# The last 256 columns of an FNet and SwiGLU kernel: SiLU, product and sum in two halves, one half's sum on GpSimd

## The chip, the cores and the metric

The kernel runs on one core of a Trainium2 chip. The metric is the device time of one execution in microseconds (us); the time given for a kernel is the median of its runs. A core has five engines that run their own instruction streams: TensorE (PE in the profile; its weight loads are PEld), VectorE (DVE), ScalarE (ACT), GpSimd (POOL) and SyncE (SP). They wait for one another on semaphores. Transfers are issued by SyncE or GpSimd (SPq and POOLq in the profile) and carried out by 16 DMA engines.

## The reference

The input x has 2048 rows (time) of 640 columns. It is normalized along its rows, goes through a Fourier mixing and through a gated feed-forward layer, and the two are multiplied and added to x:

```
xn = layernorm(x)                                            # 2048 x 640
s  = dft_seq_re @ (xn @ dft_hid_re.T) - dft_seq_im @ (xn @ dft_hid_im.T)
h  = silu(xn @ w_gate) * (xn @ w_up)                         # 2048 x 1536
g  = silu(h @ w_down)                                        # 2048 x 640
return x + s * g
```

All arrays are float32.

## The kernel before

Everything is float32, and TensorE gets each operand in two parts: a high part (ScalarE rounds it, in `split`) and a low part (VectorE takes the difference). A product of two such operands is three matmuls, high by high, high by low and low by high (`mm3`). The large products are cut into quarters and multiplied by a scheme of seven products instead of eight (`strassen`); what doesn't fit the quarters (the fifth block of 128 of the 640 columns) is computed directly, in the results named `"d1"` and `"d2"`.

The stages stand in this order at the end of the kernel's main function: four sweeps of the sequence transform (`seq`), two of the hidden transform (`hid_s`), which leave s in DRAM as `y_dram`, and then for each of two pairs of time blocks (j = 0 and 1) the gate and up products (`gate_up`) and the down product (`down`). A time block c has 512 columns of the transposed output, `out`, which is 640 x 2048.

The down product for j = 1 is the end of the kernel. There `strassen` is called with `end` set, and its last product is taken apart by the inner function `alone`: the first 256 columns of the direct block, then two banks of 512 columns for the quarter 21, then the last 256 columns of the direct block. After each of them its result is written by `result`, so that the last of these calls is `result("d2", ..., at=256, w=256)`. It handles 128 rows and 256 columns.

In `result` the buffers have the names `yb` (a piece of s, read back from `y_dram`), `res` (a piece of x, read from the transposed input `xt`) and `fin` (the piece of the output). For a direct block of j = 1 the work is: ScalarE takes SiLU of the PSUM bank into `fin` (line 1319), VectorE multiplies it by `yb` (line 1323), VectorE adds `res` (line 1330), and SyncE issues the store (line 1332). The two loads are issued by SyncE some time ahead (lines 1313 and 1315).

Nothing of this is issued where it is written. `pl.post`, `pl.prod` and `pl.step` put each instruction on a list (`Plan`) with the keys that it reads and writes, and `Plan.schedule` runs them in a planned time: matmuls (`step`) set the clock, and the others get a lane for each engine and one for all DMAs. The planner prices an instruction by its columns: columns/1183 + 0.09 us on ScalarE, columns/960 + 0.075 on VectorE, columns/500 + 0.2 on any other engine (line 92), with 0.2 us between an instruction and one that needs it. What follows a matmul (`post`) is put at its earliest time. A load (`prod`) is put as late as its first reader allows, less a reserve; loads are handled from the last to the first, and each takes the free place of the DMA lane next to its due time. The list is then sorted by planned time, and that is the order of each engine's instructions. `Plan.place` gives the buffers addresses in the arenas `hl` and `raw` by their planned lifetimes: it tries several orders and keeps the one in which buffers that follow one another at an address leave the most time between them. A buffer that is placed where another has just ended makes its first instruction wait for the other's last. All of `fin`, `yb` and `res` lie in `raw`.

All instructions of the main function are recorded under line 82 of the profile, the line of the helper through which they are issued, so groups are told apart by tile and shape.

Of the kernel before, what the change touches and what calls it, by code (L numbers as in the profile page):

```python
# [11 lines left out]
AF = mybir.ActivationFunctionType  # L12
ALU = mybir.AluOpType

P = 128
S, D, F = 2048, 640, 1536
TC = 512
# [261 lines left out]
def tile_fnet_swiglu(  # L279
# [16 lines left out]
    nc = Probe(tc.nc)  # L296
# [5 lines left out]
    pl = Plan()  # L302
# [8 lines left out]
    ps = psum.tile([P, 8, TC], F32, name="ps")  # L311
# [3 lines left out]
    def raw(name, a=0, n=None):  # L315
        o, (arena, size) = where[name], pl.size[name]
        n = size - a if n is None else n
        over = arena == "raw" and o >= RAW_KB * 256 - 8
        return space["raw3" if over else arena][:, o + a - over * (RAW_KB * 256 - 8):][:, :n]

    def hl(name, i, a=0, n=None):

        key = name, "hl"[i]
        o, n = where[key], pl.size[key][1] - a if n is None else n
        over = bisect(HL_AT, o) - 1
        return space[("hl", "hl2", "hl3")[over]][:, o + a - HL_AT[over]:][:, :n]
# [21 lines left out]
    def both(dst, *subs):  # L348
        return [(dst, p, s) for s in (subs or (0,)) for p in "hl"]
# [24 lines left out]
    def pair(b):  # L374
        return ps[:, b[0]:b[0] + len(b), :]
# [4 lines left out]
    def pkeys(b):  # L380
        return [("ps", i) for i in b]
# [6 lines left out]
    def combine(dst, b, other, op, a=0, after=0.0):  # L388
        n = len(b) * TC
        pl.post(lambda: nc.vector.tensor_tensor(wide(raw(dst, a, n)), pair(b), wide(raw(other)), op=op),  # L390
                [*pkeys(b), (other, 0)], [(dst, a)], after)
# [881 lines left out]
    def down(j):  # L1273
        names = {}

        def fetch(p, g):
            n = 768 if p[0] == "p" else 384
            name = names[p, g] = pl.buf(("Td", j, p, g), "hl", 2 * n)
            for i in range(2):
                pl.prod(14 - 4 * g, lambda i=i: nc.sync.dma_start(  # L1280
                    hl(name, i).bitcast(F32), d_dram[p, g][:, i * n:i * n + n]), [("dd", p, g, i)], [(name, "hl"[i], 0)])

        def top(p):
            for g in range(2):
                fetch(p, g)
            return (lambda g, kk, e, i: hl(names[p, g], i, kk * 256 + e * P, P)), (lambda g: both(names[p, g]))

        def dop(h):
            p = f"d{h}"
            if (p, 0) not in names:  # L1290
                for g in range(2):
                    fetch(p, g)
            return (lambda g, kk, e, i: hl(names[p, g], i, kk * P, P)), (lambda g: both(names[p, g]))

        def get(q, g):
            name = ("h", j, q % 10 - 1, q // 10)
            return name, 3 * g * TC, (name, "all", g)

        for half in range(2):
            for c in (1, 2):  # L1300
                name = ("h", j, half, c)
                for g in range(2):
                    pl.alias[name, "all", g] = [(name, (3 * g + i) * TC) for i in range(3)]

        def result(q, b, other, op, at=0, w=TC, e=0):
            half, e0 = (int(q[1]), 4) if isinstance(q, str) else (q // 10, 2 * (q % 10 - 1) + e)
            n = len(b) * w
            c = j + 2 * (half - 1)
            late = 0 if j and q in ("d2", 21) else 4
            yb, name, res = (pl.buf((what, j, q, at, e), "raw", n) for what in ("yb", "fin", "res"))  # L1310
            part = lambda ap: ap.rearrange("p (a b) -> p a b", b=w)
            fold = j == 0
            fold or pl.post(lambda: nc.sync.dma_start(
                part(raw(res)), xt[c, e0:e0 + len(b), :, at:at + w].rearrange("k p t -> p k t")), [], [(res, 0)], -8)
            pl.post(lambda: nc.sync.dma_start(
                part(raw(yb)), y_dram[c, e0:e0 + len(b), :, at:at + w].rearrange("k p t -> p k t")),
                [("yd", c, e0 + i) for i in range(len(b))], [(yb, 0)], -8)
            if other is None:
                pl.post(lambda: nc.scalar.activation(part(raw(name)), pair(b)[:, :, at:at + w], AF.Silu), pkeys(b), [(name, 0)])
            else:  # L1320
                combine(name, b, other, op)
                pl.post(lambda: nc.scalar.activation(raw(name), raw(name), AF.Silu), [(name, 0)], [(name, 0)])
            pl.post(lambda: nc.vector.tensor_tensor(raw(name), raw(name), raw(yb), op=ALU.mult),
                    [(name, 0), (yb, 0)], [(name, 0)], late)
            if fold:
                pl.post(lambda: nc.gpsimd.dma_start(
                    part(raw(name)), xt[c, e0:e0 + len(b), :, at:at + w].rearrange("k p t -> p k t"), accum_op=ALU.add),
                    [], [(name, 0)], late + 1)
            else:
                pl.post(lambda: nc.vector.tensor_tensor(raw(name), raw(name), raw(res), op=ALU.add),  # L1330
                        [(name, 0), (res, 0)], [(name, 0)], late + 1)
            pl.post(lambda: (nc.sync if j and q in ("d2", 21) else nc.gpsimd).dma_start(
                out[e0 * P:(e0 + len(b)) * P, c * TC + at:c * TC + at + w].rearrange("(k p) t -> p k t", p=P),
                part(raw(name))), [(name, 0)], [], late + 3, 8)

        strassen(("down", j), [3, 3], get, top, dop, result, j == 1)


# [83 lines left out]
```

## Time and profile before

| | |
|---|---|
| time, median of 3 runs | 969.77 us (969.72 to 969.93) |
| time of the profiled execution | 969.83 us |
| span of the profiled execution, first to last instruction | 967.6 us |
| granted TensorE clock, share of full speed | 0.999 |
| TensorE busy | 961.7 us (99%) |
| VectorE, ScalarE, GpSimd busy | 734.6, 488.6, 121.3 us |
| last matmul starts | 963.03 us |
| last store issued | 964.71 us |

Times in the profile's views are microseconds from the start of the span. A row of the timeline has an instruction's start, its duration, the engine, the line, the operation, output and input by the program's names, their number, and in brackets the idle time of the engine just before, with what ended it. A row of the groups has the number of instructions, their busy time in all and the mean duration of one in ns, then the engine's idle time before them. The chain is the work that ended last, followed back from the end to what released each step.

### The profile page before, as it was taken

Reading aid. Unit: us, or ns where it says so; the run is one execution under the profiler, and the core shown is the slowest. Engines: PE = TensorE matmul, PEld = TensorE weight load, DVE = VectorE, ACT = ScalarE, POOL = GpSimd, SP = SyncE. Lnnn points to the kernel's source line nnn. Section 1 sums busy time; section 2 is a strip of 40 time slices with the busy share of each in tenths; the row PEclk is TensorE's granted clock in tenths of the full one; section 3 lists DMA queues with packets and bytes.
Section 4 is the critical chain, followed back from the end, with each engine's and each line's share of the span. In section 5 each row is a group of like instructions: output and inputs, shape, how many; then the busy total and the mean of one; then the engine's idle time right before and its main releaser. Section 6 shows DMA issues by size and latency. Waiting matters only on the chain.

```text
span 967.6 us, 11521 instructions
## 1 busy us (share of the span) xinstructions
PE 961.7 (99%) x4235; PEld 792.0 (82%) x4235; DVE 734.6 (76%) x932; ACT 488.6 (50%) x676; POOL 121.3 (13%) x184
## 2 busy tenths in 40 slices
PE   9999999999999999999999999999999999999998
PEld 5888888888888888888888888888888888888887
DVE  7889668757774687676987898999978666666775
ACT  5686445454545455544356555563446444444341
POOL 1460211011101110111100211210002000000000
PEclk9999999999999999999999999999999999999999
DMA  9997848494938497778673374439699330105793
GB/s 352 283 249 215 233 147 229 152 271 106 231 109 255 109 236 263 208 196 253 170 213 131 141 265 155 168 136 289 222 292 256 99 133 4 55 1 163 240 346 131
DMA packets 64056, 186.50 MB, mean 193 GB/s; under 512 B 6528, under 2 KB 10368, under 8 KB 64000
## 3 DMA queue, kind: packets, MB, share of 16 engines
q1 hardware_dynamic: 45952, 125.45, 39.0%
q0 software_dynamic: 18048, 60.32, 24.2%
q8 instruction: 33, 0.54, 0.2%
q14 instruction: 23, 0.19, 0.1%
HBM read 151.39 MB, written 34.36 MB: 192 GB/s over the span
## 4 chain that ended last, share of the span: by engine, by line
PE 99%; DMA 0%; DVE 0%; ACT 0%; issue 0%; DVEq 0%; ACTq 0%
PE ps L82 99%; DMA xn<-in_x 0%; DVE raw L82 0%; DVE bst L82 0%; DVE sm L82 0%; ACT raw L82 0%; ACT sm L82 0%; DVE mv L82 0%; DVEq L82 0%; ACTq L82 0%
## 5 line engine op out<-in xcount | busy, mean ns | idle before, releaser
L82 PE MATMUL ps<-hl 128*128 128x512 f32 (+1 forms) x3258 | 780.1, 388 | 0.0
L82 PEld LDWEIGHTS ps<-hl 128*128 128x128 f32 x3258 | 610.1, 188 | 126.6 <-DVE hl L82 0.6
L82 DVE TENSOR_TENSOR hl<-raw,hl 128x1024 fp32r<-128x1024 f32 (+5 forms) x360 | 346.5, 994 | 134.3 <-ACT hl L82 94.4
L82 ACT ACTIVATE hl<-raw 128x1024 fp32r<-128x1024 f32 (+6 forms) x416 | 325.0, 826 | 170.3 <-DVE raw L82 84.8
L82 PE MATMUL ps<-hl,hl 128*128 128x512 f32 (+1 forms) x954 | 259.9, 388 | 0.0
L82 ACT ACTIVATE raw<-ps 128x512 f32<-128x512 f32 (+1 forms) x144 | 97.9, 681 | 231.4 <-PE ps L82 225.2
L82 PEld LDWEIGHTS ps<-hl,hl 128*128 128x128 f32 x954 | 179.0, 188 | 36.9
L82 DVE TENSOR_TENSOR raw<-raw 128x1024 f32<-128x1024 f32 (+7 forms) x216 | 178.6, 849 | 19.8 <-ACT raw L82 15.5
L82 DVE TENSOR_TENSOR raw<-ps,raw 128x512 f32<-128x512 f32 (+1 forms) x95 | 77.2, 814 | 48.4 <-PE ps L82 47.6
L82 DVE TENSOR_TENSOR raw<-raw,raw 128x512 f32<-128x512 f32 (+3 forms) x50 | 44.2, 892 | 6.5 <-ACT raw L82 4.3
L82 ACT ACTIVATE hl<-xn 128x1024 fp32r<-128x1024 f32 (+3 forms) x61 | 42.2, 723 | 13.6 <-PE ps L82 9.1
L82 POOL DMA_DIRECT2D p_dram<-raw x24 | 16.4, 686 | 251.4 <-DVE raw L82 215.7
L82 ACT ACTIVATE raw<-raw 128x512 f32<-128x512 f32 (+1 forms) x30 | 21.5, 718 | 46.7 <-DVE raw L82 46.7
L82 DVE TENSOR_TENSOR hl<-xn,hl 128x1024 fp32r<-128x1024 f32 (+3 forms) x50 | 40.8, 833 | 4.0 <-PE ps L82 3.9
L82 POOL DMA_DIRECT2D raw<-in_cs x36 | 32.5, 984 | 57.7 <-DMA raw<-in_cs 29.1
L82 DVE SCALAR_TENSOR_TENSOR hl<-raw,hl 128x256 fp32r<-128x256 f32 (+4 forms) x56 | 32.7, 586 | 4.0 <-ACT hl L82 4.0
L82 POOL DMA_DIRECT2D out<-raw x10 | 6.9, 689 | 226.6 <-DVE raw L82 197.3
L82 POOL DMA_DIRECT2D d_p<-hl x28 | 15.2, 543 | 71.4 <-ACT hl L82 59.6
L82 ACT ACTIVATE xn<-xn,sm,rowst 128x640 f32<-128x640 f32 (+1 forms) x16 | 14.1, 906 | 5.3 <-DVE sm L82 3.6
L82 DVE BATCH_NORM_STATS2 bst<-xn 128x6 f32<-128x320 f32 x32 | 13.7, 479 | 4.0 <-DMA xn<-in_x 4.0
L82 POOL DMA_DIRECT2D y_dram<-raw x12 | 8.2, 683 | 64.6 <-DVE raw L82 46.2
L82 POOL DMA_DIRECT2D raw<-p_dram x8 | 10.1, 1267 | 44.7 <-DVE raw L82 26.3
(42 smaller groups left out, 84.3 us busy)
## 6 DMA issues: line engine op xcount, KB each, us to landing
raw<-in_cs SPq DMA_DIRECT2D x84, 512.0 KB, 7.0
hl<-d_p SPq DMA_DIRECT2D x56, 384.0 KB, 5.0
raw<-in_cs POOLq DMA_DIRECT2D x36, 512.0 KB, 9.8
raw<-in_wb SPq DMA_DIRECT2D x24, 640.0 KB, 4.7
d_p<-hl POOLq DMA_DIRECT2D x28, 384.0 KB, 4.0
p_dram<-raw POOLq DMA_DIRECT2D x16, 512.0 KB, 4.4
raw<-p_dram SPq DMA_DIRECT2D x8, 768.0 KB, 8.5
xn<-in_x SPq DMA_DIRECT2D x16, 320.0 KB, 9.8
```

The costliest lines, as they stand in the source:

```text
L82: return real(*args, **kw)
```

## The change

In the last call of `result` (the condition `j and at` holds for no other), SiLU is taken in two halves of 128 columns, each an instruction of ScalarE out of PSUM. Each half is multiplied by its half of `yb` on VectorE. Then the first half of `res` is added on GpSimd, and the second on VectorE. The store is one, of both halves, from SyncE, and waits for both sums. The two loads and their leads, and the planned time of the store, are as before; the products and sums have no planned delay of their own any more (`late` and `late + 1` before, that is 0 and 1 us).

```diff
@@ -1315,6 +1315,19 @@
             pl.post(lambda: nc.sync.dma_start(
                 part(raw(yb)), y_dram[c, e0:e0 + len(b), :, at:at + w].rearrange("k p t -> p k t")),
                 [("yd", c, e0 + i) for i in range(len(b))], [(yb, 0)], -8)
+            if j and at:
+                m = w // 2
+                for i in range(2):
+                    pl.post(lambda a=i * m: nc.scalar.activation(
+                        raw(name, a, m), ps[:, b[0], at + a:at + a + m], AF.Silu), pkeys(b), [(name, i)])
+                for other, op in ((yb, ALU.mult), (res, ALU.add)):
+                    for i in range(2):
+                        add_on = nc.vector if other is yb or i else nc.gpsimd
+                        pl.post(lambda a=i * m, other=other, op=op, add_on=add_on: add_on.tensor_tensor(
+                            raw(name, a, m), raw(name, a, m), raw(other, a, m), op=op), [(name, i), (other, 0)], [(name, i)])
+                pl.post(lambda: nc.sync.dma_start(out[e0 * P:e0 * P + P, c * TC + at:c * TC + at + w], raw(name)),
+                        [(name, 0), (name, 1)], [], late + 3, 8)
+                return
             if other is None:
                 pl.post(lambda: nc.scalar.activation(part(raw(name)), pair(b)[:, :, at:at + w], AF.Silu), pkeys(b), [(name, 0)])
             else:
```

## The prediction

> **What bounds the kernel now.** I read the page first: the span, the busy times, the shares of the chain that ended last.
>
> ```profile
> span 967.6 us, 11521 instructions
> PE 961.7 (99%) x4235; PEld 792.0 (82%) x4235; DVE 734.6 (76%) x932; ACT 488.6 (50%) x676; POOL 121.3 (13%) x184
> PE 99%; DMA 0%; DVE 0%; ACT 0%; issue 0%; DVEq 0%; ACTq 0%
> ```
>
> TensorE sets the time. The change touches no matmul, so what it can move is what stands behind the last one. For that I read the end of the chain in order of time (start, duration, what), then SyncE's row in the timeline of the tail, the landing of that store, and what is left of the span behind it.
>
> ```profile
> 6.46 956.86 PE ps L82 x4224
> 963.32 0.02 issue
> 963.34 0.39 ACT raw L82
> 963.74 0.02 issue
> 963.76 0.44 DVE raw L82
> 964.20 0.02 issue
> 964.22 0.42 DVE raw L82
> ...
> 964.71 0.33 SPq L82 DMA_DIRECT2D out<-raw  x1
> ...
> out<-raw SPq DMA_DIRECT2D x1, 128.0 KB, 1.9
> ...
> 964.64:967.60 2.96, 0.00 (x0) 0.00 (x0) 0.00 (x1) 0.00 (x0) 0.00 (x0) 0.63 0.19 68
> ```
>
> TensorE runs one unbroken piece to 963.32. Behind it stand SiLU (963.34 to 963.73), the product (963.76 to 964.20), the sum (964.22 to 964.64), the store's issue 0.07 later at 964.71, its landing 1.9 later, and the rest of the span. So the piece that the change edits is 964.64 − 963.34 = **1.30 us**, 0.13% of the time. The 2.96 us from 964.64 on hang on the store, which stays one store of the same 128 KB; they move with it and keep their length.
>
> **The prices that the trace has.** Rows by shape (mean ns behind the busy time), then one pair of ScalarE instructions from the timeline that don't depend on each other:
>
> ```profile
> L82 ACT ACTIVATE raw<-ps 128x512 f32<-128x512 f32 x113 | 67.4, 598 | 161.0 <-PE ps L82 155.2 <-DVE raw L82 2.3 <-ACT hl L82 1.9
> L82 ACT ACTIVATE raw<-ps 128x256 f32<-128x256 f32 x2 | 0.8, 375 | 1.6 <-PE ps L82 1.6
> L82 ACT ACTIVATE hl<-xn 128x128 fp32r<-128x128 f32 x8 | 2.4, 294 | 0.0
> L82 DVE TENSOR_TENSOR raw<-raw 128x512 f32<-128x512 f32 x37 | 25.6, 691 | 14.0 <-ACT raw L82 12.8
> L82 DVE TENSOR_TENSOR raw<-raw 128x256 f32<-128x256 f32 x68 | 28.1, 419 | 2.1 <-ACT raw L82 2.0
> L82 DVE TENSOR_TENSOR hl<-xn,hl 128x128 fp32r<-128x128 f32 x8 | 2.2, 273 | 0.0
> ...
> 952.17 1.06 ACT L82 ACTIVATE raw<-raw 128x1024 f32<-128x1024 f32 x1 [7.16 <-DVE raw L82]
> 953.14 0.37 ACT L82 ACTIVATE raw<-ps 128x256 f32<-128x256 f32 x1
> ```
>
> A half costs more than half. SiLU of 128 columns out of PSUM: 598 for 512 and 375 for 256 give 0.87 ns a column and 0.26 us for 128; the nearest row of that size (from SBUF) says 0.29. I take 0.27. A product or sum of 128 on VectorE: 419 − (691 − 419)/2 = 283, the row of that size says 273; I take 0.28. Two ScalarE instructions in a row overlap by 952.17 + 1.06 − 953.14 = 0.09.
>
> **The change, part by part.** *SiLU in halves*: adds one instruction. First 963.34 to 963.61, second 963.52 (the 0.09 of overlap) to 963.79; the first half is ready 0.12 earlier than the whole was, the second 0.06 later. *Products in halves*, both on VectorE: the gap behind ScalarE is 0.03 to 0.04, so the first runs 963.65 to 963.93. The second waits for the second SiLU (963.79 + 0.03 = 963.82) and stands behind the first in VectorE's queue. What VectorE and GpSimd do to one another there is read from the one place where both work hard, about 42 us:
>
> ```profile
> 41.07 0.33 DVE L82 BATCH_NORM_AGGREGATE mv<-bst 128x2 f32<-128x12 f32 x2
> 41.49 0.18 POOL L82 TENSOR_SCALAR sm<-mv 128x2 f32<-128x2 f32 x1 [1.89 <-DVE mv L82]
> 41.76 0.72 POOL L82 TENSOR_TENSOR sm<-sm 128x2 f32<-128x2 f32 x1
> 42.55 1.23 DVE L82 TENSOR_TENSOR hl<-raw,hl 128x1024 fp32r<-128x1024 f32 x1 [1.15 <-ACT hl L82]
> 42.57 1.26 POOL L82 TENSOR_SCALAR sm<-mv 128x2 f32<-128x2 f32 x1
> 43.69 1.22 DVE L82 TENSOR_TENSOR hl<-raw,hl 128x1024 fp32r<-128x1024 f32 x1
> 43.80 1.17 POOL L82 TENSOR_TENSOR sm<-sm 128x2 f32<-128x2 f32 x1
> 44.83 1.67 DVE L82 BATCH_NORM_STATS2 bst<-xn 128x6 f32<-128x320 f32 x4
> 45.88 0.20 POOL L82 TENSOR_TENSOR sm<-sm,rowst 128x2 f32<-128x2 f32 x1
> 46.10 0.93 ACT L82 ACTIVATE xn<-xn,sm,rowst 128x640 f32<-128x640 f32 x1 [1.72 <-POOL sm L82]
> ...
> L82 POOL MEMSET z<- 128x512 bf16 x1 | 0.5, 524 | 0.3 <-POOLq L1412 0.3
> L82 POOL MEMSET sm<- 128x4 f32 x2 | 0.1, 104 | 0.0
> ```
>
> Two VectorE instructions without a wait between them overlap by 42.55 + 1.23 − 43.69 = 0.09, so the second product runs 963.84 to **964.12**; without that overlap it would run 963.95 to 964.23, which I keep as the late end.
>
> *First half's sum on GpSimd.* Three things have a row. GpSimd started 41.49 − (41.07 + 0.33) = 0.09 after VectorE released it, so it can begin at 963.93 + 0.09 = 964.02. An operation of two columns is 0.20, and ScalarE took over 46.10 − 46.08 = 0.02 after it. And it is held: the same kind of two-column scaling took 0.18 with VectorE idle and 1.26 beside a VectorE instruction with two tensors from SBUF, ending 42.57 + 1.26 − (42.55 + 1.23) = 0.05 behind it; the next one ended 43.80 + 1.17 − (43.69 + 1.22) = 0.06 behind the next such instruction. Beside the statistics, which read one tensor, it took 0.20. The second product reads two tensors and starts first (963.84 against 964.02), so I count the GpSimd sum as held to 964.12 + 0.05, and its columns after that.
>
> [...]
>
> The price of a column of a GpSimd sum has no row. Low end: the fill, (524 − 104)/508 = 0.83 ns, one write a column. High end: three such turns, two reads and a write, 2.5 ns. I take two turns, 1.65 ns: one for each of the two tensors read, with the write beside them. 126 columns beyond the two already in the row are then 0.21 us (0.10 to 0.31).
>
> [...]
>
> *Second half's sum on VectorE* is ready at 964.12 + 0.02 = 964.14 and takes 0.28. [...] If GpSimd goes first it ends at 964.17 + 0.21 = 964.38 and VectorE's ends at 964.66. If VectorE goes first, it ends at 964.42 and GpSimd's at 964.42 + 0.05 + 0.21 = 964.68. The order hardly matters: **964.66 to 964.68 against 964.64, +0.03 us**. With 0.10 to 0.31 for the columns it is 964.55 to 964.78, with the late product up to 964.89: −0.09 to +0.25.
>
> *The store* now waits for two engines. Nothing is queued behind it on SyncE. GpSimd's last work is an earlier store, and so is what SyncE did before:
>
> ```profile
> 957.11 0.72 POOL L82 DMA_DIRECT2D out<-raw  x1 [8.13 <-DVE raw L82]
> ...
> 954.94 0.87 SPq L82 DMA_DIRECT2D raw<-y_dram  x2
> 955.86 0.42 SPq L82 DMA_DIRECT2D raw<-in_xt  x1
> 963.30 0.34 SPq L82 DMA_DIRECT2D out<-raw  x1
> ```
>
> So GpSimd has been free for 6 us when the sum reaches it, and no store is behind it. The product's and the sum's other operands (y and x) are issued by 956.28, over 7 us ahead of their readers: an operand wanted 0.1 or 0.2 earlier costs nothing, and without that cover it would cost what is missing of its landing. The edits to the plan (three more instructions, no other DMA) go with this.
>
> **Sum.** Time of the profiled execution 969.83 (span 967.6 and 2.2 around it) + 0.03 = 969.86. The median of the three runs is 0.06 lower, so on its scale 969.80. I predict 969.85, between them. What a measurement here can tell from no change is about 0.2%, 1.9 us; the whole edited piece is 1.30, so not even its disappearance would show.
>
> **Rivals.**
>
> 1. *No hold.* The sums run side by side: GpSimd 964.02 + 0.20 + 0.21 = 964.43, VectorE 964.42, so 0.21 faster, 969.6. For it: VectorE's two instructions at 42 us lost nothing (1.23 and 1.22) though GpSimd worked beside them. Against it: GpSimd's own 1.26 and 1.17.
>
> 2. *Slower: GpSimd ends the chain.* Place: its sum, behind VectorE's second sum. From (964.64 − 964.47)/126 = 1.35 ns a column on, GpSimd ends later than the sum did before; it leaves the forecast's bounds once a column costs over 2.5 ns or the start takes longer than the 0.20 of the two-column rows. Upper price: the power at 41.76 took 0.72 for two columns with VectorE idle; 964.42 + 0.72 + 0.31 = 965.45, 0.8 later, 970.6. [...] Against: the other two-column rows, 0.18 to 0.20 unheld.
>
> 3. *The halves are not apart*: if the first product waits for both SiLUs, it runs 963.82 to 964.10, the second ends at 964.29, and the two sums one after the other at 964.29 + 0.26 + 0.28 = 964.83, 0.2 later, 970.0. The code names the halves apart, which speaks against it.
>
> 4. *The plan moves elsewhere.* Loads and buffers are placed by planned times, and x's due time moves by what the code's own prices give: before (0.306 + 0.2) + (0.342 + 0.2) = 1.05 behind the SiLU's start, after 0.81. If buffers of the body are placed anew and one load comes late by its whole landing, some 3 to 7 us:
>
> ```profile
> raw<-in_xt SPq DMA_DIRECT2D x1, 128.0 KB, 2.8
> raw<-in_cs SPq DMA_DIRECT2D x84, 512.0 KB, 7.0
> ```
>
> then it is 972.6 to 976.8. Against it: all that moves is at the very end.
>
> **Chances and range.** Forecast 0.55, no hold 0.20, GpSimd ends the chain 0.15, halves not apart 0.05, plan moved 0.05. The first four stay within 0.2%; of the last I give 0.03 to slower, 0.01 to faster (a buffer placed better) and the rest to no difference: faster 0.01, same 0.96, slower 0.03. The range takes in the first four: low 969.45 (0.22 below the median and the runs' spread of 0.1), high 970.6 (rival 2's upper price).
>
> **What would show it.** In the changed profile: the last matmul still at 963.0 and the one piece of TensorE unbroken; two SiLUs of about 0.27; two VectorE products of 0.28 that overlap; a GpSimd sum that ends only behind a VectorE instruction; a last sum between 964.5 and 964.9; the store's issue 0.07 behind it. The forecast is wrong if the GpSimd sum ends before the second product does, if it takes over 0.7, or if TensorE's piece has a gap that wasn't there.

## The result, and the profile after

The changed kernel takes 970.96 us (median of 22 runs, 970.84 to 971.54), the kernel before 969.83 in the same number of runs (969.52 to 970.09). The ratio is 1.0013, 95% interval 1.0007 to 1.0019: slower by 1.1 us. That is less than the 0.2% that the prediction took as what can be told from no change, but clear of the spread, and above the predicted range (969.45 to 970.6).

First the end of the chain in the changed kernel (start, duration, what; TensorE's last unbroken piece begins at 16.25 here, after a wait of 0.2 us), then three rows of its timeline: the second SiLU, GpSimd's sum and the store.

```profile
16.25 946.93 PE ps L82 x4193
963.18 0.02 issue
963.21 0.29 ACT raw L82
963.49 0.02 issue
963.52 0.20 DVE raw L82
963.72 0.01 issue
963.73 0.30 DVE raw L82
964.02 0.02 issue
964.04 0.45 DVE raw L82
```

```profile
963.38 0.27 ACT L82 ACTIVATE raw<-ps 128x128 f32<-128x128 f32 x1
...
963.90 0.44 POOL L82 TENSOR_TENSOR raw<-raw 128x128 f32<-128x128 f32 x1 [6.21 <-DVE raw L82]
...
964.56 0.33 SPq L82 DMA_DIRECT2D out<-raw  x1
```

The edited piece is as forecast: 963.21 to 964.49, that is 1.28 us against 1.30 before. GpSimd's sum ends at 964.34, VectorE's at 964.49, the store is issued 0.07 behind it. TensorE even ended 0.14 earlier in this execution. So the loss stands behind the store, where the kernel's work is over. The rows for that stand under the line of the program's end, which isn't a line of the kernel's work: L1431 in the changed kernel, L1418 in the kernel before. A row has the number of instructions, the shortest, median and longest duration in ns, and the start of the first and the last; a DRAIN stands at the end of each engine's part. The changed kernel, then the kernel before:

```profile
L1431 SPq EVENT_SEMAPHORE  x12: 17/28/28, 964.9 to 969.0; - x12
L1431 POOLq EVENT_SEMAPHORE  x4: 17/17/17, 967.9 to 969.0; - x4
L1431 POOLq DRAIN  x3: 93/188/4015, 963.9 to 968.7; - x3
L1431 SPq DRAIN  x3: 7/7/7, 966.8 to 968.1; - x3
L1431 ACTq EVENT_SEMAPHORE  x2: 17/17/17, 968.0 to 969.0; - x2
```

```profile
L1418 POOLq EVENT_SEMAPHORE  x4: 17/17/17, 966.8 to 967.5; - x4
L1418 POOLq DRAIN  x3: 46/93/5734, 957.1 to 967.2; - x3
L1418 SPq DRAIN  x3: 7/7/7, 966.7 to 967.0; - x3
L1418 ACTq EVENT_SEMAPHORE  x2: 17/17/17, 966.9 to 967.6; - x2
```

All five engines have drains under this line (in the changed kernel TensorE's weight loads from 960.9 on, ScalarE from 963.2, VectorE from 964.1). Behind the first of each come GpSimd's semaphore instructions, which I read as the collection of the engines; ScalarE's first comes 0.1 us behind GpSimd's first in both kernels (966.9 behind 966.8, 968.0 behind 967.9). In both kernels SyncE's part is done by 966.7 to 966.9, and the store has landed (1.9 behind its issue at 964.71 before, 2.1 behind 964.56 now). Before, GpSimd goes on at 966.8, at once. In the changed kernel it goes on at 967.9, since its own drain, which begins with the sum at 963.9 and takes 4.015, ends only then. The kernel before has the same drain, 5.734 long, but behind the last store that GpSimd issues, 957.1 to 962.8, under the matmuls. The 1.1 us between 966.8 and 967.9 are the 1.1 us of the result. (The span grew by 1.5, from 967.6 to 969.1. The 0.4 beyond the 1.1 lie between GpSimd's first semaphore instruction and the end, and the times of the two profiled executions do not have them: 969.83 and 970.87, 1.0 apart.)

### The profile page after: what moved, and what is told of

Its sections match the earlier page's. It is cut to its first block, busy times and chain, and to the rows that moved or that the text cites. A ratio compares the mean times of both kernels' runs of the same rounds, so it can differ in the third digit from the quotient of the medians.

```text
span 969.1 us, 11527 instructions
## 1 busy us (share of the span) xinstructions
PE 961.2 (99%) x4235; PEld 792.1 (82%) x4235; DVE 734.8 (76%) x933; ACT 488.6 (50%) x677; POOL 122.3 (13%) x185
## 4 chain that ended last, share of the span: by engine, by line
PE 98%; DMA 1%; DVE 0%; SPq 0%; ACT 0%; issue 0%
PE ps L82 98%; DMA raw<-in_cs 1%; SPq L82 0%; DVE hl L82 0%; DVE raw L82 0%; ACT xn L82 0%; ACT hl L82 0%; ACT raw L82 0%
## 5 line engine op out<-in xcount | busy, mean ns | idle before, releaser
L82 ACT ACTIVATE raw<-ps 128x512 f32<-128x512 f32 (+2 forms) x145 | 98.0, 678 | 232.3 <-PE ps L82 226.1
L82 DVE TENSOR_TENSOR raw<-raw 128x1024 f32<-128x1024 f32 (+8 forms) x217 | 178.9, 847 | 18.0 <-ACT raw L82 15.6
L82 POOL DMA_DIRECT2D raw<-in_xt x6 | 6.9, 1296 | 72.2 <-DVE raw L82 72.1
```

Of the source, the lines that this page charges most:

```text
L82: return real(*args, **kw)
```

## The experiments

Theory A: the end waits for GpSimd's closing drain, some 3.5 us behind GpSimd's last instruction. Rival B: a fetch of instructions falls into the tail because the program got longer. Rival C: the hold between VectorE and GpSimd, or a store that waits for two engines.

**The halves without GpSimd.**

```diff
-                        add_on = nc.vector if other is yb or i else nc.gpsimd
+                        add_on = nc.vector
```

> The halves as in the changed kernel, but both sums on VectorE; GpSimd's last instruction is again the store of the row at 957. Theory A (the end waits for GpSimd's closing drain, which takes some 3.5 us behind GpSimd's last instruction): that drain ends near 962.8 under the matmuls as before, the tail is 0.1 shorter than the kernel before, 969.7. Rival B (a fetch of instructions that falls into the tail because the program is longer): three instructions more as in the changed kernel, so about 970.9. Rival C (the hold between VectorE and GpSimd, or a store that waits for two engines): both are gone, 969.7; this run does not tell A from C.

Measured: 969.68 us against 969.77 (ratio 1.0001, 0.9992 to 1.0010). Its drain, the first SiLU in its chain, and the second half's sum on VectorE:

```profile
L1431 POOLq DRAIN  x3: 46/93/5742, 957.1 to 967.3; - x3
```

```profile
963.33 0.28 ACT raw L82
```

```profile
964.25 0.28 DVE L82 TENSOR_TENSOR raw<-raw 128x128 f32<-128x128 f32 x1
```

The drain is back under the matmuls and the 1.1 us are gone, with three instructions more than before: B falls for the length of the program. The packets of instructions don't go with the loss either: on queue 14 the pages count 24 in the changed kernel, 24 in this run, which lost nothing, and 23 both in the kernel before and in the next run, which lost 1.6 us. The sum takes 0.28 here and 0.45 beside GpSimd's, so the hold is there, and costs 0.17. The piece is 963.33 to 964.53, 1.20 us: the halves alone save 0.1, which the time can't show.

**A GpSimd instruction that nobody waits for.**

```diff
+            if j and at:
+                pl.post(lambda: nc.gpsimd.tensor_tensor(sm[:, 0, :2], raw(name)[:, :2], raw(name)[:, 2:4], op=ALU.add),
+                        [(name, 0)], [("idle", 0)], late + 2)
```

> The kernel before, with one GpSimd instruction of two columns behind the last sum, whose result nobody reads; the store does not wait for it. Theory A: it runs near 964.8 to 965.0, the closing drain ends some 3.5 later at 968.4, against 966.8 where SyncE is done, so the time is 1.6 to 2.0 above the kernel before: 971.4 to 971.9. Rival B: one instruction more, between no difference and 1.1: 969.8 to 970.9. Rival C: nothing on the store's path waits, 969.8.

Measured: 971.38 us (ratio 1.0016, 1.0007 to 1.0025).

```profile
964.69 0.18 POOL L82 TENSOR_TENSOR sm<-raw 128x2 f32<-128x2 f32 x1 [6.97 <-DVE raw L82]
```

```profile
L1421 POOLq DRAIN  x3: 46/102/3742, 964.7 to 968.9; - x3
L1421 SPq DRAIN  x3: 7/7/7, 966.6 to 968.7; - x3
```

Two columns that no store waits for cost 1.6 us. VectorE and the store are those of the kernel before, and SyncE is done at 966.6 (966.7 there): C falls as the cause of the loss. The drain ends at 964.66 + 3.74 = 968.40, 3.53 behind the instruction.

**A GpSimd sum earlier: first or second bank of quarter 21.**

```diff
-                pl.post(lambda: nc.vector.tensor_tensor(raw(name), raw(name), raw(res), op=ALU.add),
+                add_on = nc.gpsimd if j and q == 21 and e == 0 else nc.vector
+                pl.post(lambda: add_on.tensor_tensor(raw(name), raw(name), raw(res), op=ALU.add),
```

(`e == 1` in the second.)

> The kernel before, with the sum of the first bank of quarter 21 (512 columns, about 958.5) on GpSimd and the tail left whole. Theory A: the GpSimd sum ends near 959.8, its drain near 963.3, well before SyncE is done at 966.8: no difference, 969.8. Rival B: one instruction more on GpSimd as in the changed kernel, up to 1.1 slower, 970.9. Rival C: the hold would lengthen VectorE's work beside it, but that is under the matmuls: 969.8.

> The kernel before, with the sum of the second bank of quarter 21 (512 columns, 962.6) on GpSimd and the tail left whole. Theory A: the sum ends near 963.9, the closing drain 3.52 later at 967.4, 0.65 behind the point where SyncE is done: 970.4. Rival C (hold between the engines): the last product, 963.76, waits up to 0.1 for the GpSimd sum: 969.8 to 969.9.

Measured: 969.61 us for the first bank (ratio 0.9998, 0.9989 to 1.0007) and 970.41 for the second (1.0007, 0.9998 to 1.0016). Sum and drain of the one, then of the other, and in the other VectorE's last product, which begins while GpSimd's sum still runs:

```profile
958.61 1.28 POOL L82 TENSOR_TENSOR raw<-raw 128x512 f32<-128x512 f32 x1 [0.69 <-DVE raw L82]
```

```profile
L1419 POOLq DRAIN  x3: 46/93/4853, 958.6 to 967.3; - x3
```

```profile
962.68 1.26 POOL L82 TENSOR_TENSOR raw<-raw 128x512 f32<-128x512 f32 x1 [4.78 <-DVE raw L82]
```

```profile
L1419 POOLq DRAIN  x3: 102/188/4837, 962.6 to 968.3; - x3
```

```profile
963.84 0.43 DVE L82 TENSOR_TENSOR raw<-raw 128x256 f32<-128x256 f32 x1 [1.24 <-ACT raw L82]
```

Both drains end 3.52 behind their sum (4.853 − 1.282 and 4.837 − 1.264, less the 0.05 by which the drain's row begins before the sum's). In four kernels whose GpSimd issues the same 140 transfers the time follows the end of GpSimd's last instruction: it ends at 959.9, 963.9, 964.3 (the change) and 964.9 (the idle instruction), and the times are 969.61, 970.41, 970.96 and 971.38. By these lengths it decides from about 966.8 − 3.5 = 963.3 on; no run lies at that point. The second bank's time alone is not clear of the kernel before, since the interval takes in 1, but in its trace the drain ends at 967.5, behind SyncE, which is done at 966.9. What rival C asked for there did not come: the product took 0.43 as in the kernel before (0.43), though the first 0.11 of it stood beside GpSimd's sum.

**The last store from GpSimd.**

```diff
-            pl.post(lambda: (nc.sync if j and q in ("d2", 21) else nc.gpsimd).dma_start(
+            pl.post(lambda: (nc.sync if j and q in ("d2", 21) and not at else nc.gpsimd).dma_start(
```

> The kernel before, the last store issued by GpSimd instead of SyncE. Theory A (the end waits for GpSimd's closing drain): in the kernel before that drain ended 5.0 behind the end of GpSimd's last issue, here 964.71 + 0.72 + 5.0 = 970.4 against 966.8, so 3.7 slower, 973.4. Rival (only the store's own way counts): landing 4.5 instead of 1.9, and 0.4 more for the issue, at most 3.0 slower, and as little as 1.0 since this store is a quarter of the others: 970.8 to 972.8, with a drain that ends before the store has landed.

Measured: 972.82 us (ratio 1.0032, 1.0019 to 1.0044).

```profile
965.56 0.55 POOL L82 DMA_DIRECT2D out<-raw  x1 [7.38 <-issue]
```

```profile
L1418 POOLq EVENT_SEMAPHORE  x4: 17/17/17, 970.4 to 971.4; - x4
L1418 POOLq DRAIN  x3: 46/93/4854, 965.5 to 970.9; - x3
L1418 SPq DRAIN  x3: 7/7/117, 968.5 to 970.6; - x3
```

By the time alone the rival's upper end (972.8) fits better than the 973.4 of theory A. The rows decide: SyncE, whose longest semaphore instruction takes 3.577 us here (0.028 in the kernel before), which I read as its wait for the landing, is done at 968.7, while GpSimd's drain ends at 970.4 and GpSimd goes on only then; the rival asked for a drain that ends before the store has landed. The drain ends 4.3 behind the issue where I had 5.0. The store also went out 0.5 later than the end of the sum (965.0) explains; the cause of that stays open.

**What makes the drain long.** If it works off something that GpSimd's transfers leave behind, an earlier drain must shorten it. The changed kernel got one more drain on GpSimd, at one place each time, in the order of planned time:

```diff
+    drain_at = next(i for i, o in enumerate(pl.ops) if o[0] >= 880)
...
+        if i == drain_at:
+            tc.nc.gpsimd.drain()
```

> The changed kernel with one drain more on GpSimd in its idle stretch between about 850 and 918, so that whatever a drain clears up of GpSimd's earlier transfers is cleared there. Theory A1 (a drain has its own length of some 3.5 us whatever came before): the closing drain is as long as in the changed kernel, 970.96. Theory A2 (a drain works off what has piled up since the last one): the closing drain is much shorter, and the end waits for the store again, 969.8. Rivals B and C: as the changed kernel, 970.96.

> The changed kernel with one drain more on GpSimd near 500 us, so that some 60 of GpSimd's 140 transfers are issued after it. Behind the GpSimd sum the closing drain took 3.52 us with all 140 transfers since the last drain and 0.40 with 4. If it goes by their number, 0.31 + 60 x 0.023 = 1.7; if it goes by their packets (about 6100 of 18000), 1.4; if any earlier drain makes it short, 0.4; if it has a length of its own, 3.5. In the first three cases it ends before SyncE is done and the time is that of the kernel before, 969.7; in the last 970.96.

> The changed kernel with one drain more on GpSimd near 700 us; 14 of its transfers follow (2624 packets, 7.1 MB). Behind the GpSimd sum the closing drain took 0.40 us with 4 transfers since the last drain (512 packets, 1.8 MB) and 4.98 with 60 (some 6600 packets, 23 MB). By the number of transfers it is 0.40 + 10 x 0.082 = 1.2; by the packets 2.0; by the bytes 1.5; if a drain far enough back does nothing, 3.5. Time: it ends before SyncE is done in all cases but the last, 969.7, else 971.0.

> As the run before, the drain near 600 us; 33 transfers follow (4128 packets, 13.8 MB). Closing drain by the number of transfers 0.40 + 29 x 0.082 = 2.8; by the packets 3.1; by the bytes 2.9. It ends 0.2 to 0.6 behind the point where SyncE is done: 970.0 to 970.5.

> As the runs before, the drain near 300 us; 91 transfers follow (11828 packets, 38 MB). If the closing drain grows with all that came since the last drain, it is 7.5 us and the time 974.8. If the queue is also cleared in its own course, so that only a part is left at the end (as the 3.5 us with all 140 transfers says), it is between 0.4 and 5, and the time between 969.7 and 972.4.

> The changed kernel with one drain more on GpSimd between its last store (957) and its sum (963.9), where it runs under the matmuls, to about 962.8 as the closing drain of the kernel before does. If a drain works off what came since the last one, the closing drain behind the sum is at most 0.4, the end waits for the store again, and the time is that of the kernel before or up to 0.2 less, 969.6 to 969.8. If it has a length of its own, 970.96.

In the traces the added drains begin at 957.0 (late, behind GpSimd's last store), 755.6 (early, at the start of GpSimd's idle stretch and not between 850 and 918), 697.2, 599.3, 484.2 (midway) and 292.3. The rows of the closing drains follow in that order. The longest of the three durations is that of the closing drain; GpSimd's sum (0.44) and the 0.05 by which the row begins before it are in it.

```profile
L1434 POOLq DRAIN  x3: 34/93/563, 963.9 to 967.5; - x3
```

```profile
L1434 POOLq DRAIN  x3: 46/93/892, 964.0 to 967.6; - x3
```

```profile
L1434 POOLq DRAIN  x3: 46/102/1795, 963.6 to 967.1; - x3
```

```profile
L1434 POOLq DRAIN  x3: 46/93/3192, 964.0 to 967.9; - x3
```

```profile
L1434 POOLq DRAIN  x3: 51/93/5471, 963.6 to 969.8; - x3
```

```profile
L1434 POOLq DRAIN  x3: 51/93/2408, 964.1 to 967.9; - x3
```

| GpSimd transfers since the last drain, counted in the trace | drain behind the sum, us | time, us | ratio to the kernel before |
|---|---|---|---|
| 0 (late) | 0.07 | 969.56 | 0.9998 (0.9989 to 1.0007) |
| 4 (early) | 0.40 | 969.64 | 1.0000 (0.9991 to 1.0009) |
| 15 (700) | 1.30 | 969.48 | 0.9999 (0.9990 to 1.0008) |
| 32 (600) | 2.70 | 969.98 | 1.0002 (0.9993 to 1.0012) |
| 60 (midway) | 4.98 | 972.37 | 1.0026 (1.0016 to 1.0035) |
| 91 (300) | 1.92 | 969.49 | 0.9998 (0.9989 to 1.0007) |
| 140 (the change, no drain added) | 3.52 | 970.96 | 1.0013 (1.0007 to 1.0019) |

From 0 to 60 transfers the drain is 0.07 + 0.082 us for each: 0.40, 1.30, 2.69 and 4.99 by that line. Of the three measures that were expected to count, the number fits; by packets some 15 transfers would have taken 2.0, by bytes 1.5. With 91 and 140 it is far below the line (7.5 and 11.6), as if 23 and 42 were left. That something is also cleared in the program's own course would explain it, but is not shown; what a drain works off, and why it is shorter there, stays open. That a drain has a length of its own has fallen, and with the late drain the changed kernel keeps its GpSimd sum and is as fast as the kernel before. No version here is faster than it beyond the interval. This also shows theory A from the other side: nothing of the tail's work was touched in these six.

**Two stores.** All on VectorE, one half finished before the other is begun, a store for each half:

```diff
-                for other, op in ((yb, ALU.mult), (res, ALU.add)):
-                    for i in range(2):
+                for i in range(2):
+                    for other, op in ((yb, ALU.mult), (res, ALU.add)):
...
-                pl.post(lambda: nc.sync.dma_start(out[e0 * P:e0 * P + P, c * TC + at:c * TC + at + w], raw(name)),
-                        [(name, 0), (name, 1)], [], late + 3, 8)
+                for i in range(2):
+                    pl.post(lambda a=i * m: nc.sync.dma_start(
+                        out[e0 * P:e0 * P + P, c * TC + at + a:c * TC + at + a + m], raw(name, a, m)), [(name, i)], [], late + 3, 8)
```

> The halves with both sums on VectorE, the first half finished before the second is begun, and a store of 64 KB for each half. Theory A: GpSimd's closing drain is hidden as in the kernel before; the last sum ends 0.1 earlier than in the kernel before and the last store is half as large, so 969.4 to 969.7; one wait more of SyncE at the end (0.07) is in that. Rival: two stores cost one issue more (0.33) where they meet: 969.9.

Measured: 970.29 us (ratio 1.0006, 0.9997 to 1.0015), not the gain that I expected.

```profile
963.56 0.29 ACT raw L82
...
964.73 0.29 DVE raw L82
```

```profile
965.05 0.33 SPq L82 DMA_DIRECT2D out<-raw  x1
```

```profile
L1432 SPq DRAIN  x3: 7/7/7, 967.8 to 968.1; - x3
```

SyncE is done at 967.8, against 966.7 in the kernel before. (The profiled execution took 970.80 us, near the upper end of this version's runs.) Of the 1.1, 0.2 is TensorE, which ended that much later in this execution. Another 0.2 is the piece itself: product and sum of a half now follow one another with a wait of 0.02 between, so it takes 963.56 to 965.02, 1.46 against 1.30. The second store goes out 0.03 behind that and lands 1.8 later, at 966.9, so neither the issue nor the landing is the loss. The rest lies behind the landing: SyncE is done 0.9 later, against 0.2 in the kernel before, and in between it goes through seven more closing semaphore instructions (967.0 to 967.7). Why they stand behind the landing here stays open.

## Why the prediction was wrong

The step that failed is in the first part: "The 2.96 us from 964.64 on hang on the store, which stays one store of the same 128 KB; they move with it and keep their length." They did not: from the last sum to the end of the span it is now 964.49 to 969.1, 4.6 us. The store itself did nearly keep its length: SyncE was done at 966.9, 2.3 behind the issue, against 2.0 before (966.7 behind 964.7), and 0.2 of the difference is the landing, 2.1 against 1.9, which is 2.1 also with both sums on VectorE, where nothing was lost. But what stands behind it is, as I read the rows, the collection of all engines (GpSimd's first semaphore instruction at 966.8 before, 967.9 now), and I took the engine that came last in the kernel before for the only one that could. The same gap is in the step on the store: "So GpSimd has been free for 6 us when the sum reaches it, and no store is behind it." Its drain was behind it. The kernel before showed that drain, 5.734 us from 957.1, in the rows of the program's end, and I read no row there. The term that was missing is 967.9 − 966.8 = 1.1 us; with it the forecast of 969.85 becomes 971.0.

The other steps held in the main. SiLU of a half took 0.277 and 0.272 (0.27). The products took 0.29 and 0.28 (0.28), the second 0.20 behind the first (0.19). GpSimd began 0.09 behind the first product. GpSimd's sum ended at 964.34 and VectorE's at 964.49, against 964.24 and 964.52 when the forecast's first order (964.38 and 964.66) is moved by the 0.14 that TensorE was earlier. The whole piece is 1.28 against the forecast's 1.32.

One sum of the prediction is wrong in itself. It lets the held GpSimd sum end at 964.17 + 0.21 = 964.38, and the same sum without a hold at 964.43 (rival 1); a hold cannot make it earlier. The two-column part alone, from 964.02, lasts until 964.22, so the first order should have read 964.43 and 964.71.

That the piece came out right in spite of it is partly luck: terms inside it were off and cancelled. GpSimd's sum took 0.44, where the forecast leaves 0.36 (964.02 to 964.38), since a column costs more than my 1.65 ns: the two sums of 512 took 1.28 and 1.26, with the two-column 0.20 taken off 2.1 ns a column. And VectorE's second sum, which took 0.45 beside GpSimd's (0.28 with both sums on VectorE), ended 0.15 behind it, where the forecast has its whole 0.28 behind it: it had begun at 964.04. No run shows the forecast's two sums one wholly behind the other, in either order; here they ran beside one another for 0.30, from 964.04 to 964.34.

The forecast also had GpSimd's sum held by the second product, and it was not lengthened: 0.20 + 126 × 2.1 ns = 0.46 is my estimate of what it would take alone, and it took 0.44. The second product ran only 0.11 into it (to 964.01). Of a two-column instruction 0.15 can pass beside VectorE's, as an estimate from the rows at 42 us (0.20 alone, and an end 0.05 behind VectorE's where it is held), so 0.11 would not be felt. The run with the second bank's sum on GpSimd shows the same the other way round: VectorE's product began 0.11 before GpSimd's sum ended and kept its 0.43.

One of the signs that the prediction named for being wrong did appear, a gap in TensorE's piece that wasn't there: 0.2 us at 16.25. It has nothing to do with the loss: TensorE ended 0.14 earlier all the same, and the run with the early drain, which lost nothing, has its last unbroken piece only from 16.43 on.

Of the rivals, "no hold" falls by VectorE's 0.17 us. "GpSimd ends the chain" was right about the engine and the sign and wrong about the place: GpSimd's sum ended before VectorE's, and its price per column had little to do with it; what decides is when GpSimd's last instruction ends. "The halves are not apart" falls with the first product at 963.52, 0.03 behind the first SiLU. "The plan moves elsewhere" falls with the body, whose instructions stand in the same order on every engine, and with TensorE, which ended no later.

## What to carry to other kernels

Before work is moved to an engine that has been quiet at the end, look at what the program's end asks of that engine: the rows under the line of the program's end show each engine's closing drain. GpSimd's ended under the matmuls in the kernel before (962.8); with a sum that ended at 964.3 it ended at 967.9, behind SyncE's part (966.9), and with one that ended at 959.9 it stayed hidden (963.4). In the changed kernel it took 0.07 to 4.98 us behind GpSimd's sum, by where GpSimd had last drained. A drain of one's own behind GpSimd's last transfer, under the matmuls, brought it to 0.07 and the time back to that of the kernel before; put at 484 us instead it made the kernel slower still, 972.37. And in a tail of 1.3 us, halving saved 0.1 at best, which no run here could tell from no change.

## What the runs showed that I had not expected

In these runs GpSimd's drain behind its sum grew with the number of transfers that GpSimd had issued since the last one, 0.082 us each up to 60 (0.07 with none, 4.98 with 60), and not with their bytes, though in the traces of the kernel before and of the change the last packet of a GpSimd transfer was over by 960.0, 3.9 us before the change's sum began. With 91 and 140 transfers it was shorter than with 60 (1.92 and 3.52), which stays open.

Where a GpSimd instruction and a VectorE instruction with two tensors from SBUF meet, it was VectorE that lost here (0.45 against 0.28), while at 42 us in the kernel before GpSimd lost (1.26 against 0.18). In the one case GpSimd's instruction had begun 0.14 earlier, in the other VectorE's 0.02 earlier. In both the one that began later was lengthened; what decides it is not shown. Where the two overlapped by only 0.11, at the start of the later one, neither was lengthened (0.44 for GpSimd's sum in the change, against my estimate of 0.46 alone; 0.43 for VectorE's product behind the second bank, as in the kernel before).
